# Sixty-four leftover rows: summed with the rest, and a norm in three bf16 terms

## The chip, the cores and the metric

The kernel runs on one core of a Trainium2 chip. The metric is the device time of one execution in microseconds (us). TensorE (PE) multiplies matrices, and loads the stationary operand of each product beforehand (PEld); VectorE is called DVE, ScalarE ACT, GpSimd POOL; SyncE (SP) only issues DMAs here. POOL issues DMAs too, all those that turn fp32 into bf16 on the way.

## The reference

Two stages follow each other: an attention over channels, and a channel mix on its result.

```
B, N, C = 4, 6208, 256                      # q, k, v: [B, N, C], fp32
qn = q / (norm(q, axis=1) + 1e-6)           # norm over the N rows, one for each channel
kn = k / (norm(k, axis=1) + 1e-6)
s  = kn.transpose(0, 2, 1) @ qn / tau       # [C, C] for each batch
a  = softmax(s)                             # over the last axis
x  = v @ a                                  # [B, N, C]

x_prev = x shifted down by one row (first row zero)
xk = mu_k * x + (1 - mu_k) * x_prev
xr = mu_r * x + (1 - mu_r) * x_prev
kk = relu(xk @ w_k) ** 2                    # d_ff = 1024
out = sigmoid(xr @ w_r) * (kk @ w_v)
```

6208 rows are 12 groups of 512 rows and 64 rows more. Those 64 rows are what the change is about.

## The kernel before, in words

For each batch the kernel needs the 256 x 256 matrix of products of k and q over all rows (gathered in PSUM, `s_ps`), and the sums of squares of q and k for each channel. From these the softmax gives the matrix A of the batch, and only then can the channel mix of that batch's blocks begin. So the work is staged. A head computes the products, norms and A of batch 0, with nothing beside it. Then 49 blocks of the channel mix are worked through (48 of 512 rows, and one, "left", with the 64 leftover rows of all four batches), and the products and squares of batches 1, 2 and 3 are laid between them, each batch done before its first block is due.

A block goes through these steps: v is loaded (L403) and turned, by a DMA (L409) or, for the first five blocks, on TensorE (L421); x = v A on TensorE into `xp` (L536) and out to bf16 by ACT (L542); differences and mixes on DVE (`dl` L576, `dm` L590, `xk` and `xr` L599); up-projection (L628), relu on ACT (L632), square on DVE (L634); gate (L686) and down-projection (L693) on TensorE, tanh on ACT (L697), and the output's product on DVE (L699).

The products of a later batch run in `cov_group(b, g, key, dk)`, g being 0 to 11 for the full groups and 12 for the 64 rows. A group of 512 rows lies in SBUF as 128 partitions with four rows each. ACT squares q and k (L769), DVE adds the four rows in two steps (L772, L775) in bf16, and adds the result to `far`, an fp32 sum over groups (L779, L782). TensorE makes the products (L792, eight for a full group). Of the last full group `far` is summed over its partitions by four matmuls against a column of fp32 ones (L802, into `xp`), and DVE copies the result to `acc` (L807). The 64 rows come last: they have 64 partitions with one row each, their squares go through four bf16 matmuls of their own (also L802), and DVE adds them to `acc` (L809). POOL then takes the square root (`pow`, L287), DVE the reciprocal, and a set of six small matmuls spreads 1/|q| over partitions in three bf16 terms (L314); DVE scales the products (`e_sb`, L459), ACT takes the exponentials (L473), and DVE makes A (L480).

The order on each engine is fixed before the kernel runs. Every step is given to `Plan.add` with an engine, an estimated duration, a key (its due time, in steps of T = 9.6 us per block) and what it reads and writes. `Plan.order` then plays the steps through: an engine takes, of the steps that are ready, the one with the smallest key. So a changed step can move others. Where TensorE would idle in the head, the plan puts in matmuls on ones (`fill`, L841).

Loads of q, k and v are issued on POOL in the order of their due times, `EARLY` (three blocks) ahead at most. Each carries a gate, a wait on a certain up-projection (`after_pair`), so that they come at an even pace; loads that are due so early that no such up-projection exists had no gate, only the wait for `root0`, the square root of batch 0's norm of k. Every batch's groups are taken in the order 0 to 12 and loaded in that order, the 64 rows of q and k into the next buffer of the ring `qk`.

Of the kernel before, what the change touches and what calls it, by code (L numbers as in the profile page):

```python
# [174 lines left out]
def kernel(  # L175
# [54 lines left out]
    t2 = ring("t2", 2, [2, C])  # L230
    acc = ring("acc", 2, [4], F32)
    far = ring("far", 2, [2, C], F32)
    ones_f = sbuf("ones_f", [1], F32)
    nrm = ring("nrm", 2, [4], F32)
    rr = ring("rr", 2, [4], F32)
    rd = ring("rd", 2, [2], F32)
# [31 lines left out]
    T = 9.6  # L268

    nc.vector.memset(ones, 1.0)  # L270
    nc.vector.memset(ones_f, 1.0)
    nc.vector.memset(half, 0.5)

    def src(t, b, g):
# [60 lines left out]
    for i, (tn, g, j0, j1) in enumerate(order0):  # L335
# [2 lines left out]
        t = q if tn == "q" else k  # L338
        rows = P if g < NB else L
        n = j1 - j0  # L340
        G = qk[g]
        buf = ("qk", g, x, j0)
        if i < NF:
            f = f32s[i]
            add("SP", 0.45, key, lambda f=f, t=t, g=g: nc.sync.dma_start(f, src(t, 0, g)), writes=[("f", i)],
# [33 lines left out]
        if tn == "k":  # L379
            jq = 0  # L380
            for j in range(j0, j1):
                first = "cov" not in seen
                seen.add("cov")

                def go(G=G, g=g, j=j, rows=rows, first=first):
                    for ih in range(2):
                        nc.tensor.matmul(s_ps[:, ih, :], G[:rows, 1, j, ih * P:(ih + 1) * P], G[:rows, 0, j],
                                         start=first and ih == 0, stop=False, skip_group_check=True)
                add("PE", pe(C, 2), key + .1, go, reads=[buf, ("qk", g, 0, jq)], writes=[("s_ps",)], name="cov0")
        if i == last_q:  # L390
            kq = key + 0.6
            add("DVE", TINY, kq, lambda: nc.vector.tensor_copy(nrm[0][:, 0:2], vr[1][:, 0:2]),
# [46 lines left out]
    LEFT = NBLK - 2  # L439


    root0 = []

    def softmax(b, key):
        i = b % 2
        if b == 0:
            got = [add("DVE", TINY, key, lambda: nc.vector.tensor_copy(nrm[i][:, 2:4], vr[0][:, 0:2]),
                       reads=[("vr", 0)], writes=[("nk", i)], name="chain")]
            root0.append(inverse(i, key, nrm[i][:, 2:4], ("nk", i), 2, 4, "chain"))
        else:  # L450
            add("ACT", act(2 * C), key, lambda: nc.scalar.copy(s_sb, s_ps), reads=[("s_ps",)], writes=[("s_sb",)], name="chain s")
            inverse(i, key, acc[i], ("acc", i), 0, 4, "chain")
            m_ = spread(i, key, "chain", False)
        for ih in range(2):
            if b == 0:
                add("DVE", dve(C), key + .10, lambda ih=ih: nc.vector.tensor_tensor(e_sb[i][:, ih], s_ps[:, ih], rq, op=OP.mult),
                    reads=[("s_ps",), ("rq",)], after=got, writes=[("e", i, ih)], name="chain")
            else:
                add("DVE", dve(C), key + .10, lambda ih=ih: nc.vector.tensor_tensor(e_sb[i][:, ih], s_sb[:, ih], xp[:, :C], op=OP.mult),  # L459
                    reads=[("s_sb",)], after=[m_], give="xp" if ih else None, writes=[("e", i, ih)], name="chain")  # L460
        if shift:
            for ih in range(2):
                add("DVE", dve(C), key + .11, lambda ih=ih: nc.vector.tensor_scalar_mul(
                    e_sb[i][:, ih], e_sb[i][:, ih], rr[i][:, 2 + ih:3 + ih]), reads=[("rrk", i)], writes=[("e", i, ih)], name="chain")
            add("DVE", dve(2 * C), key + .12, lambda: nc.vector.tensor_reduce(mx[i], e_sb[i], axis=AX, op=OP.max, negate=True),
                reads=[("e", i, 0), ("e", i, 1)], writes=[("mx", i)], name="chain")
        for ih in range(2):
            def go(ih=ih):
                if shift:
                    nc.scalar.activation(e_sb[i][:, ih], e_sb[i][:, ih], AF.Exp, bias=mx[i][:, ih:ih + 1],  # L470
                                         accum_out=sm[i][:, ih:ih + 1])
                else:
                    nc.scalar.activation(e_sb[i][:, ih], e_sb[i][:, ih], AF.Exp, scale=rr[i][:, 2 + ih:3 + ih],  # L473
                                         accum_out=sm[i][:, ih:ih + 1])
            add("ACT", (0.49, 0.6), key + .13 + .01 * ih, go, reads=[("rrk", i), ("mx", i)],
                writes=[("e", i, ih), ("sm", i, ih)], name="chain exp")
        for ih in range(2):
            add("DVE", TINY, key + .15 + .01 * ih, lambda ih=ih: nc.vector.reciprocal(sm[i][:, ih:ih + 1], sm[i][:, ih:ih + 1]),
                reads=[("sm", i, ih)], writes=[("sm", i, ih)], name="chain")
            add("DVE", dve(C, 1.4), key + .155 + .01 * ih, lambda ih=ih: nc.vector.tensor_scalar_mul(  # L480
                A[b][:, ih], e_sb[i][:, ih], sm[i][:, ih:ih + 1]), reads=[("e", i, ih), ("sm", i, ih)],
                writes=[("A", b, ih)], name="chain A")

    units = []

# [257 lines left out]
        unit(kl, both)  # L743


    ng, nl = [NB + 1], [NB + 1]

    def qk_load(b, g, key, pace):
        rows, n = (P, S) if g < NB else (L, 1)
        gi = nl[0] % NG  # L750
        nl[0] += 1
        G = qk[gi]
        for x, t in enumerate((q, k)):
            add("POOL", 0.55, key + x * .001, lambda x=x, t=t: nc.gpsimd.dma_start(G[:rows, x, :n], src(t, b, g)),  # L754
                writes=[("qk", gi, x, j) for j in range(S)], size=rows * n * C * 4, name="ld qk", after=root0, gate=pace(x))

    def cov_group(b, g, key, dk):
        rows, n = (P, S) if g < NB else (L, 1)

        def work():  # L760
            gi = ng[0] % NG
            si = ng[0] % 2
            ng[0] += 1
            G = qk[gi]
            Q = sq[si]
            both = [("qk", gi, 0, 0), ("qk", gi, 1, 0)]
            sqs = [("sq", si, 0), ("sq", si, 1)]
            w = n * 2 * C
            add("ACT", act(w), key, lambda: nc.scalar.activation(Q[:rows, :, :n], G[:rows, :, :n], AF.Square), reads=both,  # L769
                writes=sqs, name="sq")  # L770
            if n == S:
                add("DVE", dve(2 * 2 * C, 2), key + .1, lambda: nc.vector.tensor_tensor(  # L772
                    t1[si], Q[:, :, 0:2], Q[:, :, 2:4], op=OP.add),
                    reads=sqs, writes=[("t1", si)], name="sum")
                add("DVE", dve(2 * C, 2), key + .2, lambda: nc.vector.tensor_tensor(t2[si], t1[si][:, :, 0], t1[si][:, :, 1], op=OP.add),  # L775
                    reads=[("t1", si)], writes=[("t2", si)], name="sum")
                F, fres = far[b % 2], ("far", b % 2)
                if g == 1:
                    add("DVE", dve(2 * C), key + .25, lambda: nc.vector.tensor_tensor(F, t2[1 - si], t2[si], op=OP.add),  # L779
                        reads=[("t2", 0), ("t2", 1)], writes=[fres], name="carry")  # L780
                elif g > 1:
                    add("DVE", dve(2 * C), key + .25, lambda: nc.vector.tensor_tensor(F, F, t2[si], op=OP.add),  # L782
                        reads=[("t2", si), fres], writes=[fres], name="carry")
                W, wres = F.rearrange("p x c -> p (x c)"), [fres]
                cols = [W[:, x * P:(x + 1) * P] for x in range(4)]
            else:
                wres = sqs
                cols = [Q[:rows, x // 2, 0, (x % 2) * P:(x % 2 + 1) * P] for x in range(4)]
            for s in range(n):
                def go(s=s):  # L790
                    for ih in range(2):
                        nc.tensor.matmul(s_ps[:, ih, :], G[:rows, 1, s, ih * P:(ih + 1) * P], G[:rows, 0, s, :],  # L792
                                         start=g == 0 and s == 0 and ih == 0, stop=g == NB and ih == 1, skip_group_check=True)
                add("PE", pe(C, 2), key + s * dk, go, reads=both, writes=[("s_ps",)], name="cov")
            if g < NB - 1:
                return
            kn = key + 1.3 * n * dk
            one = ones_f if n == S else ones

            def go():  # L800
                for x in range(4):
                    nc.tensor.matmul(xp[:, x:x + 1], cols[x], one[:rows, 0:1], start=x == 0, stop=x == 3,  # L802
                                     skip_group_check=True)
            m_ = add("PE", (0.9, 1.05) if n == S else (0.114, 0.28), kn, go, reads=wres, take="xp", name="norm")
            ai = b % 2
            if g == NB - 1:
                add("DVE", TINY, kn - 3 * T, lambda: nc.vector.tensor_copy(acc[ai], xp[:, 0:4]), after=[m_], give="xp", writes=[("acc", ai)], name="norm")  # L807
            else:
                add("DVE", TINY, kn - 3 * T, lambda: nc.vector.tensor_tensor(acc[ai], acc[ai], xp[:, 0:4], op=OP.add),  # L809
                    after=[m_], give="xp", writes=[("acc", ai)], name="norm")  # L810
        unit(key, work)


# [55 lines left out]
    start = 0.2 * T  # L869
    ends = [None, 9.2 * T, 21.0 * T, 33.0 * T]  # L870
    for b in range(1, B):
        span = (ends[b] - start) / 48.5
        for g in range(NB + 1):
            at = start + g * S * span
            cov_group(b, g, at, span)
            need.append((at, "qk", b, g))
        kb = ends[b] + .3 * T
        unit(kb, lambda b=b, kb=kb: softmax(b, kb - 4 * T))
        start = ends[b] + .35 * T
# [3 lines left out]

    def after_pair(t):
        at = [m for m in [marks.get((n, p)) for n, p in [divmod(int((t + T) / T * 4), 4)]] if m]
        return at

    need.sort()
    t = -1.6 * T
# [60 lines left out]
```

## Time and profile before

| | |
|---|---|
| median of 3 runs | 506.7 us (506.69 to 508.86) |
| the profiled execution | 506.87 us, with a span of 505.0 us on the core |
| busy PE, DVE, ACT, POOL | 486.1, 424.5, 408.0, 102.7 us |
| granted TensorE clock | full in all of the span |
| traffic | 78.7 MB read from HBM, 25.4 MB written |
| fp32 norm matmuls (L802), 3 batches | 24 passes, 2.9 us busy |
| bf16 norm matmuls of the 64 rows (L802) | 12, 0.7 us busy |
| fp32 sums over groups (L782) | 30, 20.6 us busy on DVE |

The span is what the core's trace covers, from the first instruction to the last; 1.9 us of the execution's time lie outside it. In the profile an engine's busy time counts overlapping instructions once, a row in brackets names what ended an idle time, and names such as `far` stand for all buffers of a ring. A matmul on fp32 operands shows as two passes, so four matmuls are eight rows. Some matmul records are missing from a trace.

### The profile page before, as it was taken

The page shows a single profiled execution, that of the slowest core. Times are in us where ns is not written, and L with a number is a line of the kernel's source. Part 1 is how long each engine was busy: PE and PEld are TensorE (multiplying, and loading weights), DVE is VectorE, ACT ScalarE, POOL GpSimd, SP SyncE. Part 2 cuts the span into 40 slices and gives each one's busy share as a digit, 9 for nine tenths or more (in the row PEclk, how much of TensorE's full clock was granted, in tenths as well). Part 3 has the DMA queues.
Part 4 walks back from the last instruction along what each step waited for, and adds up shares of the span by engine and source line. Part 5 has one row for each costly group of instructions (what it writes and reads, how often), then busy time and mean ns, then how long its engine had stood idle before and what let it go on. Part 6 is the DMA issues. An engine that isn't in the chain of part 4 may idle for free.

```text
span 505.0 us, 9492 instructions
## 1 busy us (share of the span) xinstructions
PE 486.1 (96%) x3477; PEld 357.3 (71%) x3536; DVE 424.5 (84%) x979; ACT 408.0 (81%) x582; POOL 102.7 (20%) x174
## 2 busy tenths in 40 slices
PE   2999999999999999999999999999999999999997
PEld 0366777777777777777776777777777777777785
DVE  4569899999899989998879999899779787878974
ACT  6867998898889888888789888888767777777774
POOL 6552222223231211222121122211110111000000
PEclk9999999999999999999999999999999999999999
DMA  9999999999999999999897999995654786542113
GB/s 209 209 205 202 152 135 162 177 228 169 214 180 143 200 180 213 180 157 179 137 176 123 185 175 160 185 169 98 142 109 84 136 123 127 103 105 63 53 75 105
DMA packets 96294, 77.36 MB, mean 153 GB/s; under 512 B 49588, under 2 KB 77944, under 8 KB 96248
## 3 DMA queue, kind: packets, MB, share of 16 engines
q0 software_dynamic: 41776, 38.84, 56.2%
q1 hardware_dynamic: 54472, 37.92, 37.5%
q8 instruction: 27, 0.44, 0.3%
q14 instruction: 19, 0.16, 0.1%
HBM read 78.71 MB, written 25.43 MB: 206 GB/s over the span
## 4 chain that ended last, share of the span: by engine, by line
PE 86%; DMA 6%; DVE 5%; issue 2%; ACT 0%; POOL 0%; DVEq 0%; ACTq 0%; POOLq 0%
PE vr L693 32%; PE kT L628 30%; PE xp L536 8%; PE vr L686 8%; PE s_ps L792 6%; DMA qk<-in_q_dram 3%; DMA v_bf<-in_v_dram 2%; DMA qk<-in_k_dram 2%; DVE kk L634 1%; DVE dl L576 1%; DVE dm L590 1%; PE kT L841 0%; ACT kr L632 0%; DVE xk L599 0%; DVE res L699 0%
## 5 line engine op out<-in xcount | busy, mean ns | idle before, releaser
L632 ACT ACTIVATE kr<-kT 128x1024 bf16<-128x1024 f32 (+1 forms) x200 | 199.7, 1001 | 51.8 <-PE kT L628 45.9
L628 PE MATMUL kT<-xk,w_k 128*128 128x512 bf16 (+1 forms) x742 | 201.2, 372 | 2.8
L693 PE MATMUL vr<-w_v,kk 128*128 128x256 bf16 x1536 | 202.2, 273 | 0.1
L634 DVE TENSOR_TENSOR kk<-kr 128x1024 bf16<-128x1024 bf16 (+1 forms) x200 | 134.1, 671 | 45.3 <-ACT kr L632 45.1
L693 PEld LDWEIGHTS <-kk 128*128 128x128 bf16 x1552 | 169.1, 112 | 3.8 <-DVE kk L634 0.4
L628 PEld LDWEIGHTS <-w_k 128*128 128x128 bf16 x800 | 77.6, 98 | 51.6 <-issue 1.5
L697 ACT ACTIVATE res<-vr 128x256 f32<-128x256 f32 x192 | 74.4, 388 | 12.2 <-PE vr L693 8.5
L699 DVE SCALAR_TENSOR_TENSOR res<-res,vr 128x256 f32<-128x256 f32 x192 | 79.4, 414 | 2.9 <-ACT res L697 2.7
L686 PE MATMUL vr<-w_r,xr 128*128 128x256 bf16 x384 | 73.4, 273 | 0.0
L769 ACT ACTIVATE sq<-qk 128x2048 bf16<-128x2048 bf16 (+1 forms) x39 | 70.6, 1811 | 2.1 <-DMA qk<-in_k_dram 1.4
L542 ACT CAST xR<-xp 128x512 bf16<-128x512 f32 x94 | 55.3, 588 | 13.5 <-PE xp L536 12.7
L403 POOL DMA_DIRECT2D v_bf<-in_v_dram x48 | 36.2, 754 | 146.1 <-PE kT L628 139.1
L686 PEld LDWEIGHTS <-xr 128*128 128x128 bf16 x384 | 42.7, 112 | 30.3 <-issue 0.2
L590 DVE TENSOR_SCALAR dm<-dl,mu 128x512 bf16<-128x512 bf16 (+1 forms) x192 | 59.0, 346 | 0.4
L536 PE MATMUL xp<-vT,A 128*128 128x512 bf16 x188 | 55.9, 379 | 0.5
L792 PE MATMUL s_ps<-qk 128*128 128x256 bf16 (+1 forms) x294 | 55.0, 273 | 0.1
L754 POOL DMA_DIRECT2D qk<-in_q_dram x39 | 20.8, 533 | 97.5 <-ACT res L697 32.4
L792 PEld LDWEIGHTS <-qk 128*128 128x128 bf16 (+1 forms) x294 | 28.5, 98 | 14.6 <-issue 0.6
L576 DVE TENSOR_TENSOR dl<-xR 128x1024 bf16<-128x1024 bf16 (+1 forms) x49 | 33.1, 676 | 0.8 <-ACT xR L542 0.6
L754 POOL DMA_DIRECT2D qk<-in_k_dram x39 | 20.8, 533 | 62.9 <-PE kT L628 42.1
L599 DVE TENSOR_TENSOR xk<-dm,xR 128x1024 bf16<-128x1024 bf16 x47 | 32.5, 691 | 0.9
L599 DVE TENSOR_TENSOR xr<-dm,xR 128x1024 bf16<-128x1024 bf16 x47 | 32.3, 687 | 0.4
(94 smaller groups left out, 259.1 us busy)
## 6 DMA issues: line engine op xcount, KB each, us to landing
out_dram<-res SPq DMA_DIRECT2D x47, 512.0 KB, 4.9
v_bf<-in_v_dram POOLq DMA_DIRECT2D x48, 256.0 KB, 6.8
qk<-in_k_dram POOLq DMA_DIRECT2D x47, 256.0 KB, 7.9
qk<-in_q_dram POOLq DMA_DIRECT2D x46, 256.0 KB, 7.7
res<-in_q_dram SPq DMA_DIRECT2D x2, 512.0 KB, 4.3
vT<-v_bf SPq DMA_TRANSPOSE x43, 7.5
w_k<-in_moe_w_k_dram POOLq DMA_DIRECT2D x1, 512.0 KB, 9.5
w_v<-in_moe_w_v_dram POOLq DMA_DIRECT2D x1, 512.0 KB, 9.5
```

Of the source, the lines that this page charges most:

```text
L536: nc.tensor.matmul(xp, A[b][:, ih, dh * P:(dh + 1) * P], vT[o].rearrange("p (s h) q -> p h s q", h=2)[:, ih], start=ih == 0, stop=ih == 1)
L590: unit(km, lambda col=col, dh=dh, c0=c0, c1=c1, km=km, w=w: add("DVE", dve(w, 2.77), km, lambda: nc.vector.tensor_scalar_mul(dm[di][:, dh, ...
L599: nc.vector.tensor_tensor(o[which][:, :, c0:c1], dm[di][:, :, c0:c1], xR[:, :, at + c0:at + c1], op=OP.add)
L628: last = nc.tensor.matmul(kT[bk][:, x, :w], w_k[:, dh, fh * P:(fh + 1) * P], xk[n % 2][:, dh, c0:c1], start=dh == 0, stop=dh == 1)
L632: add("ACT", act(2 * w), ku + .1, lambda: nc.scalar.activation(kr[kri][:, :, :w], kT[bk][:, :, :w], AF.Relu, scale=0.5 ** 0.5), reads=[("k ...
L634: add("DVE", dve(2 * w, 2), ku + .2, lambda: nc.vector.tensor_tensor(kk[n % 2][:, 2 * p:2 * p + 2, c0:c1], kr[kri][:, :, :w], kr[kri][:, : ...
L686: nc.tensor.matmul(V[:, D:], tokens(xr[ri][:, dh]), w_r[:, dh, :], start=dh == 0, stop=dh == 1)
L693: nc.tensor.matmul(V[:, :D], tokens(kk[n % 2][:, fh]), w_v[:, fh, :], start=fh == 0, stop=fh == 7)
L697: add("ACT", act(D), kd + .3, lambda: nc.scalar.activation(r[:, s], V[:, D:], AF.Tanh, scale=0.5), reads=[bank], writes=[("res", oi, s)], ...
L699: add("DVE", dve(D), kd + .4, lambda: nc.vector.scalar_tensor_tensor(r[:, s], r[:, s], 1.0, V[:, :D], op0=OP.add, op1=OP.mult), reads=[ban ...
L769: add("ACT", act(w), key, lambda: nc.scalar.activation(Q[:rows, :, :n], G[:rows, :, :n], AF.Square), reads=both, writes=sqs, name="sq")
L792: nc.tensor.matmul(s_ps[:, ih, :], G[:rows, 1, s, ih * P:(ih + 1) * P], G[:rows, 0, s, :], start=g == 0 and s == 0 and ih == 0, stop=g == ...
```

## The change

- The 64 rows have a buffer of their own, `qkl`, whose other 64 partitions are zeroed once, by POOL, among the head's loads. Their two products (formerly over 64 partitions) now run over all 128 partitions.
- In every batch the 64 rows come third (0, 1, 12, 2, ...), in the order of the loads and in that of the work, and the step between the groups' due times is 1/49 of the batch's stretch instead of 1/48.5.
- Their squares go to `sql`, and one DVE operation on 64 partitions adds them to `far`. The four matmuls of their own and the add to `acc` are gone.
- After the last full group `far` is split on DVE into three bf16 terms: a copy to bf16, the rest by an fp32 subtraction, a copy of the rest, and what is then left. Twelve bf16 matmuls (three terms by four columns' blocks, one column wide) replace the four fp32 ones, against the bf16 ones that exist already.
- Loads for which no up-projection was found as a gate (`after_pair`) now wait for the last DVE operation of batch 0's A (`am`, the second of L480).

The head keeps its own code for batch 0, with the 64 rows in `qkl`. The core of the diff:

```diff
@@ sbuf
-    ones_f = sbuf("ones_f", [1], F32)
+    qkl = sbuf("qkl", [2, 1, C])
+    sql = sbuf("sql", [2, C])
+    terms = ring("terms", 3, [2, C])
...
@@ softmax
+            if b == 0:
+                am.append(a_)
...
-    ng, nl = [NB + 1], [NB + 1]
+    ng, nl = [NB], [NB]
+    add("POOL", 0.4, HK + 6, lambda: nc.gpsimd.memset(qkl[L:], 0.0), writes=[("qkl0",)], name="zero")
...
@@ qk_load
-        nl[0] += 1
-        G = qk[gi]
+        nl[0] += g < NB
+        G = qk[gi] if g < NB else qkl
...
@@ cov_group
             else:
-                wres = sqs
-                cols = [Q[:rows, x // 2, 0, (x % 2) * P:(x % 2 + 1) * P] for x in range(4)]
+                G, both = qkl, [("qkl", 0), ("qkl", 1), ("qkl0",)]
+                add("ACT", act(2 * C), key, lambda: nc.scalar.activation(sql[:L], qkl[:L, :, 0], AF.Square), reads=both, writes=[("sql",)], name="sq")
+                add("DVE", dve(2 * C), key + .25, lambda: nc.vector.tensor_tensor(F[:L], F[:L], sql[:L], op=OP.add),
+                    reads=[("sql",), fres], writes=[fres], name="carry")
...
-            if g < NB - 1:
+            if g != NB - 1:
                 return
             kn = key + 1.3 * n * dk
-            one = ones_f if n == S else ones
+            h, m, l = terms
+            for x, (o, a, r) in enumerate(((h, F, None), (F, F, h), (m, F, None), (l, F, m))):
+                add("DVE", dve(2 * C, 1.4 if r is None else 1.0), kn - 3 * T, (lambda o=o, a=a: nc.vector.tensor_copy(o, a)) if r is None else
+                    (lambda o=o, a=a, r=r: nc.vector.tensor_tensor(o, a, r, op=OP.subtract)), reads=[fres], writes=[fres] + ([("terms",)] if o is not F else []), name="terms")

             def go():
-                for x in range(4):
-                    nc.tensor.matmul(xp[:, x:x + 1], cols[x], one[:rows, 0:1], start=x == 0, stop=x == 3,
-                                     skip_group_check=True)
+                for t_ in range(3):
+                    W = terms[t_].rearrange("p x c -> p (x c)")
+                    for x in range(4):
+                        nc.tensor.matmul(xp[:, x:x + 1], W[:, x * P:(x + 1) * P], ones[:, 0:1], start=x == t_ == 0, stop=x == 3 and t_ == 2, skip_group_check=True)
...
-        span = (ends[b] - start) / 48.5
-        for g in range(NB + 1):
-            at = start + g * S * span
+        span = (ends[b] - start) / 49
+        at = start
+        for g in [0, 1, NB] + list(range(2, NB)):
             cov_group(b, g, at, span)
             need.append((at, "qk", b, g))
+            at += (S if g < NB else 1) * span
...
@@ after_pair
-        return at
+        return at or am[-1:]
```

More of the change, by code (lines that the diff above doesn't have):

```diff
@@ L270 @@
     nc.vector.memset(ones, 1.0)
-    nc.vector.memset(ones_f, 1.0)
     nc.vector.memset(half, 0.5)
@@ L340 @@
         n = j1 - j0
-        G = qk[g]
-        buf = ("qk", g, x, j0)
+        G = qk[g] if g < NB else qkl
+        buf = ("qk", g, x, j0) if g < NB else ("qkl", x)
         if i < NF:
@@ L388, in go @@
                                          start=first and ih == 0, stop=False, skip_group_check=True)
-                add("PE", pe(C, 2), key + .1, go, reads=[buf, ("qk", g, 0, jq)], writes=[("s_ps",)], name="cov0")
+                add("PE", pe(C, 2), key + .1, go, reads=[buf, ("qk", g, 0, jq) if g < NB else ("qkl", 0)], writes=[("s_ps",)], name="cov0")
         if i == last_q:
@@ L439 @@
     LEFT = NBLK - 2
-    root0 = []
+    root0, am = [], []
     def softmax(b, key):
@@ L479, in softmax @@
                 reads=[("sm", i, ih)], writes=[("sm", i, ih)], name="chain")
-            add("DVE", dve(C, 1.4), key + .155 + .01 * ih, lambda ih=ih: nc.vector.tensor_scalar_mul(
+            a_ = add("DVE", dve(C, 1.4), key + .155 + .01 * ih, lambda ih=ih: nc.vector.tensor_scalar_mul(
                 A[b][:, ih], e_sb[i][:, ih], sm[i][:, ih:ih + 1]), reads=[("e", i, ih), ("sm", i, ih)],
                 writes=[("A", b, ih)], name="chain A")
+            if b == 0:
+                am.append(a_)
     units = []
@@ L750, in qk_load @@
         gi = nl[0] % NG
-        nl[0] += 1
-        G = qk[gi]
+        nl[0] += g < NB
+        G = qk[gi] if g < NB else qkl
         for x, t in enumerate((q, k)):
             add("POOL", 0.55, key + x * .001, lambda x=x, t=t: nc.gpsimd.dma_start(G[:rows, x, :n], src(t, b, g)),
-                writes=[("qk", gi, x, j) for j in range(S)], size=rows * n * C * 4, name="ld qk", after=root0, gate=pace(x))
+                writes=[("qk", gi, x, j) for j in range(S)] if g < NB else [("qkl", x)], size=rows * n * C * 4, name="ld qk", after=root0, gate=pace(x))
     def cov_group(b, g, key, dk):
@@ L760, in work @@
         def work():
[L761 to L771, printed above, removed]
+            gi, si = ng[0] % NG, ng[0] % 2
+            F, fres = far[b % 2], ("far", b % 2)
+            if g < NB:
+                ng[0] += 1
+                G, Q = qk[gi], sq[si]
+                both = [("qk", gi, 0, 0), ("qk", gi, 1, 0)]
+                sqs = [("sq", si, 0), ("sq", si, 1)]
+                add("ACT", act(n * 2 * C), key, lambda: nc.scalar.activation(Q, G, AF.Square), reads=both, writes=sqs, name="sq")
                 add("DVE", dve(2 * 2 * C, 2), key + .1, lambda: nc.vector.tensor_tensor(
@@ L776, in work @@
                     reads=[("t1", si)], writes=[("t2", si)], name="sum")
-                F, fres = far[b % 2], ("far", b % 2)
                 if g == 1:
@@ L783, in work @@
                         reads=[("t2", si), fres], writes=[fres], name="carry")
-                W, wres = F.rearrange("p x c -> p (x c)"), [fres]
-                cols = [W[:, x * P:(x + 1) * P] for x in range(4)]
-            else:
-                wres = sqs
-                cols = [Q[:rows, x // 2, 0, (x % 2) * P:(x % 2 + 1) * P] for x in range(4)]
+            else:
+                G, both = qkl, [("qkl", 0), ("qkl", 1), ("qkl0",)]
+                add("ACT", act(2 * C), key, lambda: nc.scalar.activation(sql[:L], qkl[:L, :, 0], AF.Square), reads=both, writes=[("sql",)], name="sq")
+                add("DVE", dve(2 * C), key + .25, lambda: nc.vector.tensor_tensor(F[:L], F[:L], sql[:L], op=OP.add),
+                    reads=[("sql",), fres], writes=[fres], name="carry")
             for s in range(n):
@@ L791, in go @@
                     for ih in range(2):
-                        nc.tensor.matmul(s_ps[:, ih, :], G[:rows, 1, s, ih * P:(ih + 1) * P], G[:rows, 0, s, :],
-                                         start=g == 0 and s == 0 and ih == 0, stop=g == NB and ih == 1, skip_group_check=True)
+                        nc.tensor.matmul(s_ps[:, ih, :], G[:, 1, s, ih * P:(ih + 1) * P], G[:, 0, s, :],
+                                         start=g == 0 and s == 0 and ih == 0, stop=g == NB - 1 and s == S - 1 and ih == 1, skip_group_check=True)
@@ L800, in go @@
             def go():
-                for x in range(4):
-                    nc.tensor.matmul(xp[:, x:x + 1], cols[x], one[:rows, 0:1], start=x == 0, stop=x == 3,
-                                     skip_group_check=True)
[L804 to L810, printed above, removed]
+                for t_ in range(3):
+                    W = terms[t_].rearrange("p x c -> p (x c)")
+                    for x in range(4):
+                        nc.tensor.matmul(xp[:, x:x + 1], W[:, x * P:(x + 1) * P], ones[:, 0:1], start=x == t_ == 0, stop=x == 3 and t_ == 2, skip_group_check=True)
@@ L811, in cov_group @@
+            m_ = add("PE", (0.37, 0.5), kn, go, reads=[("terms",)], take="xp", name="norm")
+            add("DVE", TINY, kn - 3 * T, lambda: nc.vector.tensor_copy(acc[b % 2], xp[:, 0:4]), after=[m_], give="xp", writes=[("acc", b % 2)], name="norm")
         unit(key, work)
```

## The prediction

> **What bounds the kernel now.** I read the page's busy times first, then the windows of the engines, then TensorE's timeline around the work that the change touches, last the timeline of the head (the time up to the first block).
>
> ```profile
> span 505.0 us, 9492 instructions
> ...
> PE 486.1 (96%) x3477; PEld 357.3 (71%) x3536; DVE 424.5 (84%) x979; ACT 408.0 (81%) x582; POOL 102.7 (20%) x174
> ...
> PE 86%; DMA 6%; DVE 5%; issue 2%; ACT 0%; POOL 0%; DVEq 0%; ACTq 0%; POOLq 0%
> ```
>
> TensorE carries 86% of the chain that ended last. The windows (PE, PEld, DVE, ACT, POOL) say how full each stretch is:
>
> ```profile
> 55.00:80.00 25.00, 24.84 (x183) 18.68 (x184) 24.39 (x55) 23.75 (x29) 6.29 (x11) 1.00 1.19 150
> ...
> 41.00:380.00 339.00, 336.24 (x2410) 251.25 (x2454) 303.21 (x682) 288.30 (x403) 73.69 (x122) 1.00 1.10 167
> ```
>
> From 41 us TensorE hardly stops: what leaves its stream shortens the span, what is added elsewhere costs nothing until it makes TensorE wait. DVE has 339.0 - 303.2 = 35.8 us free in this stretch, but only 0.6 of the 25 us after 55.
>
> **TensorE: what goes and what comes.** The norms at the end of batch 1, with the work around them:
>
> ```profile
> 142.74 0.95 PE L802 MATMUL xp<-ones_f,far 128*128 128x1 f32 x8
> 143.54 0.38 PE L792 MATMUL s_ps<-qk 128*128 128x256 bf16 x2
> ...
> 144.29 0.25 PE L802 MATMUL xp<-ones,sq 64*128 64x1 bf16 x4
> 144.47 0.63 PE L693 MATMUL vr<-w_v,kk 128*128 128x256 bf16 x4
> ```
>
> Busy spans overlap, so the price is from start to start. The four fp32 matmuls run as eight passes: 143.54 - 142.74 = 0.80 us. The four of the tail: 144.47 - 144.29 = 0.18. Batch 3 shows 0.81 and 0.18. Batch 2 shows 1.03 for the fp32 set, but the group behind it has three matmuls where the code issues pairs; one of 0.22 us lacks its record, which leaves 0.81. Both sets of all three batches: 3 x (0.81 + 0.18) = 2.97 us.
>
> New are twelve bf16 matmuls of one column per batch, each with a weight load of its own. The nearest row is the end of the head:
>
> ```profile
> 35.40 0.34 PE L376 MATMUL vr<-ones,sq 128*128 128x1 bf16 x8
> ```
>
> One lasts 0.16, so eight start within 0.34 - 0.16 = 0.18, or 0.025 each. Twelve cost the tail's 0.18 for four plus 8 x 0.025 = 0.38; three batches 1.14. The other end is 12 x 0.056 = 0.67 per batch (six matmuls of 128 columns on fresh weights take 0.34 us at 149.50), 2.0 in all. I take 1.14, the same form. Net -1.83 us (-0.96 at the other end). Covariance matmuls keep their number, and 64 or 128 rows cost the same (274 and 273 ns).
>
> A rule speaks against this saving. The Trainium skill ("TensorE: Matmul & The Clock Gate", Back-to-back issue gap) gives about 81 ns per load and matmul at 128 columns, sustained, and says that the bare gap leaves out the weight load. The trace does not agree: 56 ns at 128 columns, 25 at one, with weight loads. By the rule's 81 ns a batch would pay 0.97 and the net would be -0.06 us, by an estimate from that page.
>
> **DVE: what comes, and its cover.** Per batch two fp32 to bf16 copies, two subtractions and one add over 512 columns. Adds of this size (L782) last 0.69 and stand 0.60 apart (69.53 to 70.13); casts took 0.69 for 1024 columns (L347) and 0.35 for 256 (L480), so about 0.46 for 512, 0.38 apart. Sum: 2 x 0.38 + 3 x 0.60 = 2.56, less one tiny add (0.07): 2.5 us per batch, 7.5 in all, into 35.8 us of free time. In the changed order the four split operations stand between blocks' work well ahead of the twelve matmuls (9, 27 and 24 DVE operations lie between the last split and the copy of the norm out of PSUM, L807, which are 4.5 us in batch 1 by their rows), so the matmuls find them ready. The cover of the chain behind: counted in TensorE's own column time, from norm to the spread of 1/|q| (L314) it was 5.1, 3.7 and 4.8 us from the tail's norm and is 5.5, 5.5 and 4.8 from the new set's start; from spread to the first product with the new A (L536) it was 5.3, 4.2, 4.0 and is 3.8, 4.1, 4.2. Batch 1 is the tight one: from e_sb (L459) to the second A, DVE's order holds, by the spacing of their rows, 0.66 + 0.33 (L699) + 0.60 (L634) + 0.07 + 0.34 (L775) + 0.26 + 0.07 + 0.33 + 0.34 = 3.0 us, and e_sb began 0.7 behind the spread (149.50 to 150.20): 3.7 of 3.8. I take no stall, and 0.5 as the bound.
>
> Before has stalls of its own: TensorE waits 0.27 us at 265.4 for xk (L599), which DVE reached late behind the softmax of batch 2; the changed order puts that block's xk elsewhere. The windows leave 2.8 us up to 380 in which TensorE was not busy, unrecorded matmuls among them. I take none of it as gained; it is the other bound.
>
> **Head and loads.** The first loads of batch 1 now wait for the last A of batch 0 (L480). What they did there:
>
> ```profile
> 36.79 2.10 PE L841 MATMUL kT<-ones 128*128 128x512 bf16 x9
> 37.80 0.76 POOL L403 DMA_DIRECT2D v_bf<-in_v_dram  x1
> 38.00 0.67 DVE L480 TENSOR_SCALAR A<-e_sb,sm 128x256 bf16<-128x256 f32 x1
> 38.74 0.28 PE L513 MATMUL kT<-vT,A 128*128 128x256 bf16 x1
> 38.77 0.35 DVE L480 TENSOR_SCALAR A<-e_sb,sm 128x256 bf16<-128x256 f32 x1
> 39.18 0.28 PE L513 MATMUL kT<-vT,A 128*128 128x256 bf16 x1
> ```
>
> The first A took 0.67 where the others take 0.35, beside a DMA issue of POOL. The Trainium skill ("SBUF — State Buffer", Who interferes with whom) has POOL and such one-source DVE operations lock each other out; here that is one operation, while 34 of L590 beside an issue stayed within 383 ns (median 348). Removing it frees 0.32 us of DVE and nothing of TensorE: nine fill matmuls at 0.216 keep it until 38.73, and the first half's four products at 0.109 until 39.17, just where A's halves were ready. The order keeps those fills, and is the same on TensorE up to about 52 us. I take 0, bounded by 0.3 either way (the held issues fall beside the cast L523 at 39.61).
>
> Behind the new wait on POOL stand q and k of the first group and v of block 3: issued from about 38.9 instead of 36.69, landing 7.7 us later by 49. They are wanted at 54.78 (L769) and at 53.75 (turn of v3), and that turn is placed 3 us later; the next load stands behind an up-projection anyway (42.32). The zeroing of 64 rows x 512 on POOL costs about 0.7 (0.26 for 128 columns, 0.12 for 2) in the head's loads and ends inside the 0.80 that POOL waited at 7.42. Loads of the last rows move from last to third in each batch, same bytes: 0.
>
> **Sum.** 506.87 us (the profiled execution: span 505.0 and 1.9 around it) - 1.83 = 505.04; the median of the runs is 0.17 lower: 504.9 us, -0.36%. A difference within 0.5% (2.5 us) is about what a measurement of this kernel can tell from none.
>
> **Rivals.** (1) More comes back: the 0.27 at 265.4 and a fifth of the other 2.5 us not busy go too, the order being laid anew: 1.83 + 0.77 = 2.6 us, 504.1. For it: nearly all waits sit around the batches' ends, which are re-laid. Against: nothing in the change aims at them.
> (2) Slower: DVE is full in one place, the 25 us after 55, where the early add of the last rows (0.6) now falls among the turned v, sums and squares; there, and at each split, DVE falls behind, kk and the gate's result come late, and TensorE waits. At the full price 7.5 - 1.8 = +5.7 us, 512.4; it decides above 2.5 us from the point where 4.4 of the 7.5 us (58%) reach TensorE. For: 24.39 of 25 us busy. Against: 35.8 us free over the whole stretch, and TensorE never waited there. By the lock rule of the Trainium skill named above, each of six new casts could also wait out a DMA issue.
> (3) The new weight loads aren't hidden: with one column there is nothing to hide a load behind. One lasts 0.098 us (L387), twelve 1.18, three batches 3.5: 3.5 - 2.97 = +0.6, 507.3. Against: eight starts within 0.18 us at 35.40. This is the Trainium skill's weight load rule above, at the trace's own duration.
>
> **Chances.** The sum 0.44, (1) 0.30, (2) 0.20, (3) 0.06. Of the sum's chance 0.08 lies beyond -2.5 us, of (1) a quarter falls short of it, of (2) 0.03 ends below +2.5: faster 0.08 + 0.22 = 0.30, slower 0.17, same the other 0.53. Likeliest case alone: 504.1 to 506.0. Range: 503.4 (1.83, half of the 2.8 not busy, and 0.1 for the runs) to 508.4 (a third of the DVE time on the path, with the head's 0.3, the softmax's 0.5 and 0.2 for the runs), leaving out most of (2).
>
> **What the profile after would show.** Right: no fp32 matmul on TensorE, bursts of twelve that end 0.38 us after their start, DVE near 432 us busy, no PE wait above 0.3 us named by the waits, first POOL load behind 38.8, first up-projection at 41.2 as before, last matmul 1.8 us earlier. Wrong: L628 or L693 waiting on L634 in 55 to 80 us, L536 waiting for A at 154, 265 or 383, a burst of 0.7 us or more, or a head that moved.

## The result

The changed kernel takes 503.38 us (median of 6 runs, 503.17 to 503.57) against 506.74 before: 3.36 us or 0.66% less by the medians. The ratio of the runs is 0.9925, with a 95% interval of 0.991 to 0.9939, so it is faster. The forecast, 504.9 in a range of 503.4 to 508.4, had the sign and a little over half of the size; the median lies 0.02 us below the range. The profiled execution took 503.57 us, with a span of 501.8: 3.2 us less than before's span, and this difference is accounted for below. (In most kernels here, the one before too, some executions last 1 to 7 us longer than the rest, which are called undisturbed below; where a profile or a median below is one of the long ones, the text gives the single times.)

The page of the changed kernel, its busy times and the shares of the chain that ended last:

```profile
span 501.8 us, 9553 instructions
...
PE 486.3 (97%) x3536; PEld 356.0 (71%) x3536; DVE 430.4 (86%) x990; ACT 406.2 (81%) x582; POOL 104.8 (21%) x175
...
PE 90%; DMA 5%; DVE 2%; POOL 1%; issue 0%; ACT 0%; POOLq 0%
```

DVE's busy time grew by 5.9 us and TensorE's share of the chain from 86% to 90%: TensorE is the bound more than before. The windows (PE, PEld, DVE, ACT, POOL) of the changed kernel in the two stretches shown of before:

```profile
55.00:80.00 25.00, 25.00 (x191) 18.84 (x190) 24.47 (x52) 22.36 (x30) 6.65 (x11) 1.00 1.18 175
41.00:380.00 339.00, 338.73 (x2478) 252.28 (x2476) 312.59 (x703) 289.51 (x410) 75.39 (x123) 1.00 1.04 167
```

TensorE is busy for all but 0.3 of the 339 us; DVE has 26.4 of its 35.8 free microseconds left. (This trace has all 800 records of the up-projection, the one of before 742; part of the 2.8 us that looked idle before was missing records.)

TensorE's timeline around the norm of batch 1, where before had two sets of norm matmuls:

```profile
142.01 0.59 PE L631 MATMUL kT<-xk,w_k 128*128 128x512 bf16 x2
142.44 0.44 PE L807 MATMUL xp<-ones,terms 128*128 128x1 bf16 x12
142.75 0.38 PE L792 MATMUL s_ps<-qk 128*128 128x256 bf16 x2
```

From start to start the twelve take 142.75 - 142.44 = 0.31 us (0.303 by the unrounded starts, in all three batches), where the fp32 set alone took 0.80. And this is the changed kernel's product of the 64 rows in batch 1, over 128 partitions:

```profile
62.57 1.03 PE L631 MATMUL kT<-xk,w_k 128*128 128x512 bf16 x4
63.43 0.38 PE L792 MATMUL s_ps<-qkl 128*128 128x256 bf16 x2
63.65 0.61 PE L422 MATMUL kT<-ident,v_bf 128*128 128x128 bf16 x8
```

Four matmuls of 512 columns at 0.216 make 0.86, and the products start just then (63.43); the two take 63.65 - 63.43 = 0.22. In the trace of before the same two took longer, which the prediction did not see. The rows there, over 64 partitions, and the weight loads beside them:

```profile
138.18 1.04 PE L693 MATMUL vr<-w_v,kk 128*128 128x256 bf16 x8
139.15 0.39 PE L792 MATMUL s_ps<-qk 64*128 64x256 bf16 x2
139.47 1.04 PE L628 MATMUL kT<-xk,w_k 128*128 128x512 bf16 x3
```

```profile
138.84 0.11 PEld L693 LDWEIGHTS <-kk 128*128 128x128 bf16 x1
139.15 0.11 PEld L792 LDWEIGHTS <-qk 64*128 64x128 bf16 x2 [0.20 <-issue]
139.47 0.11 PEld L628 LDWEIGHTS <-w_k 128*128 128x128 bf16 x2 [0.21 <-issue]
```

Eight matmuls of 256 columns at 0.109 end their streaming at 139.05, but the next starts at 139.15; and the two take 139.47 - 139.15 = 0.32 instead of 0.22. Each change of the row count, 128 to 64 and 64 to 128, leaves a gap of just under 0.1 us, and the second matmul behind each change comes another 0.01 late (0.01 to 0.03 around the norm sets): by the unrounded starts 0.21 us around the products of a batch. Durations don't show it (273 and 274 ns), and since busy spans overlap, neither do busy times and windows; starts do.

So the 3.2 us of the span fall into these parts, all from starts in the two traces:

| part | us | in the forecast |
|---|---|---|
| fp32 norm sets gone (3 x 0.81), twelve bf16 matmuls come (3 x 0.30) | -1.53 | -1.29 |
| norm sets of the 64 rows gone (3 x 0.18) | -0.54 | -0.54 |
| the gap ahead of each of those sets and the late second matmul behind it (3 x (0.096 + 0.027)) | -0.37 | not seen |
| gaps on both sides of the 64 rows' products (3 x 0.21) | -0.63 | 0 |
| wait near 265 us, 0.27 to 0.14 | -0.13 | 0 |
| first up-projection at 41.07 instead of 41.18 | -0.11 | 0 |
| short delays that are new: 0.07 at batch 1's product with the new A, the rest 0.02 each | +0.14 | 0 |
| sum | -3.17 | -1.83 |

### The profile page after: what moved, and what is told of

It reads as the page before. It is cut to its first block, busy times and chain, and to the rows that moved or that the text cites. A ratio compares the mean times of both kernels' runs of the same rounds, so it can differ in the third digit from the quotient of the medians.

```text
span 501.8 us, 9553 instructions
## 1 busy us (share of the span) xinstructions
PE 486.3 (97%) x3536; PEld 356.0 (71%) x3536; DVE 430.4 (86%) x990; ACT 406.2 (81%) x582; POOL 104.8 (21%) x175
## 4 chain that ended last, share of the span: by engine, by line
PE 90%; DMA 5%; DVE 2%; POOL 1%; issue 0%; ACT 0%; POOLq 0%
PE vr L696 33%; PE kT L631 33%; PE vr L689 8%; PE xp L539 8%; PE s_ps L792 6%; DMA qk<-in_q_dram 2%; DMA v_bf<-in_v_dram 2%; DMA qk<-in_k_dram 2%; POOL qk L351 1%; PE kT L840 0%; DVE kk L637 0%; DVE xk L587 0%; PE kT L696 0%; DVE xr L587 0%; DVE dl L579 0%
## 5 line engine op out<-in xcount | busy, mean ns | idle before, releaser
L631 PE MATMUL kT<-xk,w_k 128*128 128x512 bf16 (+1 forms) x800 | 206.7, 373 | 0.2
L700 ACT ACTIVATE res<-vr 128x256 f32<-128x256 f32 x192 | 74.5, 388 | 14.3 <-PE vr L696 11.0
L772 ACT ACTIVATE sq<-qk 128x2048 bf16<-128x2048 bf16 x36 | 68.7, 1908 | 0.0
L792 PE MATMUL s_ps<-qk 128*128 128x256 bf16 x288 | 54.0, 273 | 0.0
L792 PEld LDWEIGHTS <-qk 128*128 128x128 bf16 x288 | 28.1, 98 | 16.1
L758 POOL DMA_DIRECT2D qk<-in_q_dram x36 | 19.4, 540 | 73.9 <-ACT res L700 17.7
L773 DVE TENSOR_TENSOR t<-sq 128x1024 bf16<-128x1024 bf16 x36 | 24.7, 687 | 10.6 <-ACT sq L772 10.6
```

Of the source, the lines that this page charges most:

```text
L631: last = nc.tensor.matmul(kT[bk][:, x, :w], w_k[:, dh, fh * P:(fh + 1) * P], xk[n % 2][:, dh, c0:c1], start=dh == 0, stop=dh == 1)
L700: add("ACT", act(D), kd + .3, lambda: nc.scalar.activation(r[:, s], V[:, D:], AF.Tanh, scale=0.5), reads=[bank], writes=[("res", oi, s)], ...
L772: add("ACT", act(n * 2 * C), key, lambda: nc.scalar.activation(Q, G, AF.Square), reads=both, writes=sqs, name="sq")
L792: nc.tensor.matmul(s_ps[:, ih, :], G[:, 1, s, ih * P:(ih + 1) * P], G[:, 0, s, :], start=g == 0 and s == 0 and ih == 0, stop=g == NB - 1 a ...
```

## The experiments

Theory S (switch) says that the unforeseen part is the row count: a matmul with 64 rows of weights among ones with 128 costs a gap on the way in and one on the way out. Theory O (order) says that rows cost nothing and the new order took waits away. Theory H gives a part to the held loads. Every ratio is to the kernel before, timed beside the run on the same chip. Where medians are too wide to tell two kernels apart, TensorE's stream is compared: the time from the start of the first up-projection to the start of the last matmul, by the unrounded starts of the traces. It is 456.93 us in the changed kernel's profile and 456.91 in the one of its last repeat, so these two undisturbed executions agree within 0.02 us; before it was 460.01.

**The changed kernel again, and only the products' rows undone.**

> The changed kernel once more, as the measure for the others of its company. Every theory: 503.4 us, 3.35 us below the kernel before.

Measured: 503.73 us median (503.32 to 507.08; ratio 0.994, 0.9916 to 0.9964). Four of six runs lie within 503.32 to 503.77.

```diff
-  matmul(s_ps[:, ih, :], G[:, 1, s, ih * P:(ih + 1) * P], G[:, 0, s, :], ...)
+  matmul(s_ps[:, ih, :], G[:rows, 1, s, ih * P:(ih + 1) * P], G[:rows, 0, s, :], ...)
```

> The changed kernel, but the six products of the 64 rows (two in each of batches 1 to 3) run over 64 partitions again, not over the zeroed 128; the order is the same on every engine. Theory S (switch: a matmul with 64 rows of weights among ones with 128 costs about 0.10 us more on going in and 0.09 on coming back, because its weight load isn't taken ahead): 3 x 0.19 = 0.57 us slower than the changed kernel, 504.0, with a gap of about 0.20 us from the 256-column matmul ahead to the first of them. Theory O (order: rows cost nothing, 274 against 273 ns, and what came beyond the sum is waits that the new order took away): no difference, 503.4.

Measured: 504.07 us median (four of six within 503.96 to 504.07; ratio 0.9944, 0.9924 to 0.9963). That is 0.3 above the median of the changed kernel beside it, and 0.4 between the undisturbed runs of the two; the intervals don't separate them, the trace does. TensorE's timeline and then its weight loads, in this run:

```profile
62.48 1.03 PE L631 MATMUL kT<-xk,w_k 128*128 128x512 bf16 x4
63.44 0.39 PE L792 MATMUL s_ps<-qkl 64*128 64x256 bf16 x2
63.76 0.62 PE L422 MATMUL kT<-ident,v_bf 128*128 128x128 bf16 x8
```

```profile
62.92 0.10 PEld L631 LDWEIGHTS <-w_k 128*128 128x128 bf16 x1
63.44 0.11 PEld L792 LDWEIGHTS <-qkl 64*128 64x128 bf16 x2 [0.42 <-issue]
63.76 0.45 PEld L422 LDWEIGHTS <-v_bf 128*128 128x128 bf16 x8 [0.21 <-issue]
```

62.48 + 0.86 = 63.34, so the products start 0.10 late, and they take 0.32: all of the gap is back, with the same order on every engine. It is there in all three batches (63.3, 157.2 and 275.6 us): 3 x 0.21 = 0.63 us. TensorE's stream agrees: 457.55 us, 0.62 longer than in the changed kernel. The second fence shows what goes with it: the load of 64 rows starts with its matmul (63.44), and the one of 128 rows behind it with its own (63.76). In the changed kernel the loads of the same tiles run ahead of their matmuls:

```profile
63.22 0.31 PEld L792 LDWEIGHTS <-qkl 128*128 128x128 bf16 x2
63.54 0.54 PEld L422 LDWEIGHTS <-v_bf 128*128 128x128 bf16 x8
```

There the load of 63.22 stands 0.21 ahead of its matmul at 63.43. S holds, O falls for this part. Why a load of another row count isn't taken ahead, no run here shows.

**The switch by itself, 144 times.** A matmul of zeros goes between the two halves of every product of a full group; the twins differ in its rows alone and have the same order.

```diff
+  if ih == 0 and g < NB:
+      matmul(s_ps[:, 0, 0:1], zer[:128, 0:P], zer[:128, 0:1], start=False, stop=False)   # zero128
+      matmul(s_ps[:, 0, 0:1], zer[:64, 0:P], zer[:64, 0:1], start=False, stop=False)     # zero64 instead
```

> The changed kernel with a matmul of zeros between the two halves of every covariance step of the full groups in batches 1 to 3 (144 of them: 128 rows of zero weights, one column, added to the products, which it doesn't change). The measure for its twin of 64 rows. Every theory: 144 x 0.025 = 3.6 us more, 507.0.

> The same kernel with the same order on every engine, but the matmuls of zeros take 64 rows of zero weights instead of 128. Theory S: each costs 0.096 on going in and 0.092 until the next, 0.188 instead of 0.025: 144 x 0.163 = 23.5 us more than its twin, 530.5. Theory O (rows cost nothing): the same as its twin, 507.0.

Measured: 506.94 us for 128 rows (ratio 1.0003, 0.9984 to 1.0022), 534.02 for 64 rows (1.0531, 1.0515 to 1.0547). The difference is 27.1 us, or 0.188 for each insertion; 23.5 was expected. One of them on TensorE, 64 rows and then 128 rows:

```profile
100.53 0.27 PE L794 MATMUL s_ps<-qk 128*128 128x256 bf16 x1
100.73 0.17 PE L797 MATMUL s_ps<-zer 64*128 64x1 bf16 x1
100.84 0.28 PE L794 MATMUL s_ps<-qk 128*128 128x256 bf16 x1
```

```profile
101.52 0.27 PE L794 MATMUL s_ps<-qk 128*128 128x256 bf16 x1
101.63 0.17 PE L797 MATMUL s_ps<-zer 128*128 128x1 bf16 x1
101.66 0.27 PE L794 MATMUL s_ps<-qk 128*128 128x256 bf16 x1
```

Over all 144 the median step from the product ahead to the matmul of zeros is 0.205 us against 0.109, and the step from there to the next product 0.106 against 0.028. These make 0.174; the step behind that is 0.011 longer too. By these steps an insertion adds 0.213 us with 64 rows and 0.028 with 128: half the rows cost more than seven times the time when they stand alone between others. This settles S for 64 rows against 128; other row counts were not run.

**One part of the change alone, in the kernel before.** The 64 rows get their zeroed buffer, and products, squares and norm run over 128 partitions. They stay last, with their own norm set.

```diff
+  if g == NB:
+      G, Q, both, sqs = qkl, sql, [("qkl", 0), ("qkl", 1), ("qkl0",)], [("sql",)]
-  activation(Q[:rows, :, :n], G[:rows, :, :n], AF.Square)
+  activation(Q[:, :, :n], G[:, :, :n], AF.Square)
-  matmul(s_ps[:, ih, :], G[:rows, 1, s, ...], G[:rows, 0, s, :])     # and the norm's cols, one[:rows]
+  matmul(s_ps[:, ih, :], G[:, 1, s, ...], G[:, 0, s, :])             # and the norm's cols, one[:]
```

> The kernel before with one part of the change alone: the 64 rows in a buffer of their own, zeroed to 128 partitions, so that products, squares and norm of the 64 rows run over 128 partitions; they stay last, the fp32 norm set, the split norm and the loads' gates stay as before. Theory S: 12 switches less, 6 going in at 0.096, 3 back from products at 0.093, 3 back from norms at 0.067: 1.07 us, 505.7. Theory O: 506.7, unless its slightly changed order shows other waits.

Measured: inconclusive by the median, 507.32 us (ratio 0.9994, 0.9977 to 1.0012). Of twelve runs three took 505.4 to 505.8, as S expects, and the others 506.1 to 508.8. Its profiled execution is one of the three (505.8), and there the gap is gone: the products take their place 0.22 us long, and TensorE's stream is 458.63 us, 1.38 less than before (S expected 1.07). So the padding alone shortens the stream, but not the median of this kernel. Why it runs longer so often wasn't found.

**The held loads, given free.**

```diff
-  return at or am[-1:]
+  return at
```

> The changed kernel without the new gate of the first loads. The prediction's reading (A comes 0.3 us earlier on DVE, but the fill matmuls keep TensorE until then): no difference to the changed kernel, 503.4, with the first A at about 0.67 us again. Theory H (the 0.1 us that the first up-projection came earlier, and more behind it, is the held loads' work): 0.1 to 0.4 us slower, 503.5 to 503.8.

Measured: 503.51 us median (nine of twelve within 503.34 to 503.75; ratio 0.9949, 0.9924 to 0.9973): no difference to the changed kernel. The profile is of one of the long runs (506.73), whose waits come later (from 109 us on); the head bears on the question here. POOL, DVE and TensorE in it:

```profile
37.52 0.76 POOL L404 DMA_DIRECT2D v_bf<-in_v_dram  x1
37.72 0.68 DVE L481 TENSOR_SCALAR A<-e_sb,sm 128x256 bf16<-128x256 f32 x1
38.45 0.28 PE L516 MATMUL kT<-vT,A 128*128 128x256 bf16 x1
```

In the changed kernel the first A takes 0.35 at 37.95 and the product starts at 38.64:

```profile
37.95 0.35 DVE L481 TENSOR_SCALAR A<-e_sb,sm 128x256 bf16<-128x256 f32 x1
38.64 0.27 PE L516 MATMUL kT<-vT,A 128*128 128x256 bf16 x1
39.10 0.58 POOL L758 DMA_DIRECT2D qk<-in_q_dram  x1 [2.42 <-DVE A L481]
```

Without the hold A takes 0.68 again, and the fills on TensorE hide it. H falls; the 0.11 us of the head are within what the head varies between runs (the first up-projection started between 40.77 and 41.24 us in the profiles of these kernels, at 40.90 in this one).

**The fp32 set back.** The split is left out of DVE, and `far` goes through four fp32 matmuls.

```diff
-  for t_ in range(3): ... matmul(xp[:, x:x + 1], W[:, x * P:(x + 1) * P], ones[:, 0:1], ...)
+  W = F.rearrange("p x c -> p (x c)")
+  for x in range(4): matmul(xp[:, x:x + 1], W[:, x * P:(x + 1) * P], ones_f[:, 0:1], ...)
```

> The changed kernel, with one part undone: the sum of squares goes through four fp32 matmuls again (eight passes of 0.11 us) and isn't split on DVE; all else of the change stays. By the rows of the changed kernel's trace the twelve bf16 matmuls take 0.30 us per batch and the fp32 set took 0.81: 3 x 0.51 = 1.5 us slower than the changed kernel, 504.9. A theory in which the split's DVE work costs TensorE time would make it less than that, or faster than 503.4.

Measured: 505.03 us median (nine of twelve within 504.82 to 505.53; ratio 0.9978, 0.9951 to 1.0006), some 1.5 us above the undisturbed runs of the changed kernel on the other chips (on this chip it was not run): the row that the sum started from, with 0.30 in place of 0.38 for the new set. TensorE's stream is 1.38 us longer than in the changed kernel; the rows give 1.52, less the wait near 265 us, which this run doesn't have.

**The split on DVE, twice.** Four more DVE operations per batch, into spare tiles.

```diff
+  for o, a, r in ((spare, F, None), (sparf, F, spare), (spare, sparf, None), (sparf, sparf, spare)):
+      add("DVE", ...)   # tensor_copy or subtract, as the split itself
```

> The changed kernel with the split done twice (four more DVE operations per batch, into spare tiles; the first result isn't used). If DVE's free time covers the split, as the prediction's sum has it: 503.4. If added DVE work reaches TensorE (the prediction's second rival): up to 3 x 1.96 = 5.9 us more, 509.3, and 506.4 at half of it.

Measured: 503.73 us (503.56 to 503.98; ratio 0.993, 0.9918 to 0.9941), about 0.3 above the changed kernel on the other chips (on this chip it was not run). The window of 41 to 380 us, as above:

```profile
41.00:380.00 339.00, 338.74 (x2476) 252.06 (x2475) 317.05 (x715) 288.72 (x410) 75.17 (x123) 1.00 1.06 167
```

DVE is busy 4.5 us longer than in the changed kernel. TensorE's stream is 0.32 us longer, in short waits between 147 and 160 us, near the softmax of batch 1: of the 5.9 us at stake in the forecast of this run, about a twentieth reached TensorE. The prediction's second rival, with most of DVE's new time on the path, has no ground here.

**A version a little below both.** Two terms instead of three; then, besides, the 64 rows seventh instead of third.

```diff
-  ((h, F, None), (F, F, h), (m, F, None), (l, F, m))      # three terms
+  ((h, F, None), (m, F, h))                               # two; matmuls for t_ in range(2)
-  for g in [0, 1, NB] + list(range(2, NB)):
+  for g in list(range(6)) + [NB] + list(range(6, NB)):    # two_late only
```

> The changed kernel with two bf16 terms of the sum of squares instead of three (the third, at most 2 to the power -16 of the sum, is left out): four matmuls of 0.025 us and two DVE operations less per batch. TensorE's sum: 3 x 0.10 = 0.3 us less than the changed kernel, 503.1, if it takes 503.4 here. If DVE's time mattered it would be more.

> The same, with the 64 rows taken seventh (behind six full groups) instead of third, so that ACT no longer has to square the next batch's 64 rows, which wait for their load, ahead of a softmax's exponentials. TensorE's work is the same: 503.1 in undisturbed executions. If the late load of the 64 rows is what makes some executions 3 to 4 us longer (14.3 us to landing in the profile of one of 507.1), there are fewer of those; if other transfers do it, as many.

> The changed kernel once more, as the measure for these two: 503.4 us, 1 to 2 of 6 executions some 3 us longer.

Measured: 503.23 us with two terms (ratio 0.9929, 0.9907 to 0.9951), 503.14 with the other place too (0.9929, 0.9904 to 0.9955), 503.47 for the changed kernel beside them (0.9926, 0.991 to 0.9942). The step of 0.24 is about the 0.3 of the rows, but these ratios can't tell them apart. One of six runs of each new version was long (506.27 and 507.02), none of the changed kernel here: the place of the 64 rows is not shown to matter for that. Two long executions of kernels with the 64 rows third left profiles: the first repeat of the changed kernel (507.08) and the kernel without the hold (506.73). In the first ACT waits for the next batch's 64 rows, and TensorE for A behind that:

```profile
152.53 0.63 ACT L786 ACTIVATE sql<-qkl 64x512 bf16<-64x512 bf16 x1 [4.27 <-DMA qkl<-in_k_dram]
...
154.49 0.39 PE L539 MATMUL xp<-vT,A 128*128 128x512 bf16 x1 [2.60 <-DVE A L481]
```

A load issued at 138.19 landed 14.3 us later, ACT's square of it stands ahead of the softmax's exponentials, and TensorE lost 2.6 us. In the changed kernel's own profile this square ran at 148.21 without a wait. In the second the load of the 64 rows is late too, but TensorE's longest wait there (2.0 us, until 157.70) goes back to another load: ACT stands at the square of a full group, whose k was issued at 140.26 and landed 14.9 us later. In both executions every load issued from 138 to 148 us, of q, k, v and the 64 rows, took 11.7 to 15.6 us to land, against 2.4 to 9.0 in the changed kernel's own profile. So the stretch is slow for all loads, not for the 64 rows alone. What slows it is open.

## Why the prediction was right or wrong

Wrong above all in one term: "64 or 128 rows cost the same (274 and 273 ns)". That compared durations, in a paragraph that had just said to price from start to start, since busy spans overlap. By starts, the rows of before show 0.21 us per batch around the products and 0.12 around each norm set of the 64 rows: 1.0 us in three batches, of the 1.34 by which the span beat the sum. The term was priced at nothing without naming the gap; the weight loads of before would have shown it, as the 64-row load starts only with its matmul (139.15). The runs that undo it (0.62 us in the trace) and multiply it (27 us) show the cause.

The term of the new set was too high: 0.38 per batch, built on the tail's 0.18 for four matmuls. That 0.18 held a switch back to 128 rows (0.092 where the others take 0.025); without one, twelve cost 0.30. It is the same misreading once more, worth 0.24 us.

Right: the fp32 sets at 0.81 each, as the run with fp32 shows; that DVE's work has cover, as the doubled split shows within 0.3 us; that the head and the held loads give nothing, as the run without the hold shows. Batch 1's chain was the tight one: it lost 0.07 us at its product with the new A. The wait near 265 us shrank by 0.13, half of the 0.27 that the first rival gave back there; the rest of the 2.8 us not busy, of which that rival took a fifth and the range half, was in part missing records.

The two places of the Trainium skill: its 81 ns for a load and a matmul ("TensorE: Matmul & The Clock Gate", Back-to-back issue gap) would have left no gain; the changed trace has 36 pairs of one column at 25 ns and pairs of 128 columns (L422) at 56, so the measurement stands against it here. Its lock between POOL and one-source DVE operations like the one that makes A ("SBUF — State Buffer", Who interferes with whom) agrees with the first A at 0.68 us beside an issue of POOL and 0.35 without; other A's that overlapped an issue took 0.34 to 0.45, so it is not seen each time. It changes nothing in the time here.

The chances put 0.30 on faster by over 0.5%, which is what came. The first rival's 504.1 came nearest in size, by another mechanism than its own: of its returned waits only 0.13 us came. Where the chances and that rival were near, it was by luck.

## What to carry to other kernels

Price a matmul from its start to the next one's start, and where its row count differs from its neighbours', count the gap on both sides: a leftover of 64 rows among 128-row matmuls was dearer on TensorE than the same rows padded with zeros. (The padding by itself did not lower the median in the kernel before, so the rest of the schedule has to be looked at too.) Where TensorE is the bound and another engine has free time in the same stretch, the fp32 operand of a reduction on TensorE can be split into bf16 terms on that engine; whether that engine has room is tested by doubling its new work.

## What the runs showed of the hardware that was not expected

Between 128-row matmuls, weights of 64 rows aren't loaded ahead: the load began with its own matmul, 0.096 us after the stream could have gone on, and the next load of 128 rows again didn't run ahead (0.106 us from a one-column matmul to the next, instead of 0.028). Among themselves the four 64-row matmuls of the norm stood 0.025 apart, the second 0.039 behind the first: it is the change that costs, not the 64 rows. Only 64 against 128 rows was measured, with the 64 in the first 64 partitions.
